# Per-head attention weights from a DRAM scratch, coarser loads and stores, and a reordered end, in a forward-and-backward kernel

## Chip, cores and metric

The kernel runs on one core of a Trainium2 chip. The metric is the device time in microseconds (us) of one execution. All data are bf16 in DRAM; sums are kept in f32 in PSUM.

## What is computed

The kernel computes a gated block and all its gradients, in one launch. With x of 2048 rows and D = 576 columns, 32 heads of 128 columns and 2048 cached keys and values per head:

```python
xn = layernorm(x)                                    # no affine part
q  = (xn @ wq) per head;  p = softmax(q @ K^T / sqrt(128));  o = p @ V
s  = concat(o) @ wo                                  # attention, 2048 x 576
g  = silu((sigmoid(xn @ w_gate) * (xn @ w_up)) @ w_down)   # MLP, inner size 4608
out = x + s * g
# and the gradients of out for x, K, V, wq, wo, w_gate, w_up, w_down, given grad_out
```

B_x is an input that the reference doesn't use.

## The kernel before

Rows are worked on in 16 tiles of 128 (`NT`, index `st` or `qt`); D = 576 is five tiles (`DT`), of which the last has 64 columns. Where weights lie with D on the partitions, this last tile is padded (`KPAD`): the 64 real rows lie in the upper half of the partitions, the lower half is zero. The stages follow each other on the one core:

1. MLP forward (lines 340 to 490): for 80 row steps (5 groups of columns of w_gate and w_up, 16 row tiles each; the first group is one chunk of 512 columns, the others two) TensorE makes `g_ps` and `u_ps`, ScalarE the sigmoid into `a_row`, VectorE the product into `h_row`. GpSimd stores both to DRAM (`h_d`, `a_d`, lines 472 and 473), with four buffers each. Beside it run the *guard* pieces (lines 249 to 281): SyncE loads K and wq into `x_all`, seven pieces ahead, and VectorE and ScalarE in turn square and sum them. They decide later whether the fast branch of attention, which has no row maximum, is safe. The order of this stage is written out by hand (`manual_schedule`).
2. The down projection (lines 505 to 548) and what is needed for the gate; the first head is prepared there too: `prep_kt`, `prep_wot` (TensorE turns wo of head 0 by five transposes) and `prep_qt`.
3. Attention, forward and backward, head by head (lines 594 to 868). A head has 32 slots: 16 of `main1` (scores, exponential, and a transpose of the row tile by DMA on SyncE, `PT`) and 16 of `main2` (dP, dS, and its transpose, `dST`). The tails `tail1` and `tail2` come six slots later and make O and dq, the sums over row tiles for dV and dK (`Partial`, line 744) are spread over the slots. `plan(h)` puts every other piece of work at a slot with `put`; a list scheduler then orders the instructions of each engine. GpSimd issues all plain loads and stores: per head K and V in quarters (line 177), wq in two loads (`load_wq`, 512 + 64 rows of 256 bytes), wo in two loads (`load_wo`), O and dq in stores of four row tiles each (`store_nat`, `G4 = 4`, lines 674 to 677). SyncE issues all DMA transposes: PT and dST, K and V (`turn_nat`), and wo of the next head (`turn_wot`, line 208), which lies in the single buffer `wo_h`.
4. The output product (lines 905 to 983): O of one row tile, turned by a DMA transpose (`load_oT`, line 584), times wo, whose rows have been loaded into dead buffers. Three buffers for the turned O, `oTs`, lie in KQ, in the rest of xnT and in `xn_all`. The loads of the second and third are held back by a one-element copy on GpSimd out of a row that was just loaded:

```python
loads[0] = row_loads(0)
for st in range(1, R0):
    nc.gpsimd.tensor_copy(oTs[st][0:1, 0, 0:1], loads[0][st % 3][0:1, 0:1])
    load_oT(oTs[st], st)
```

   TensorE works in the order: row tile 0 with those wo rows that are there early, row tile 1 with the same, row tile 0 with the late wo rows (those in Kn, Vn and dOn), then row tile 2, and so on.
5. The backward pass of the MLP in 18 blocks of 256 columns (lines 1055 to 1160).
6. The gradients of wq and wo and of xn through q, in eight groups of four heads (lines 1206 to 1262, `hg` = 0 to 7). A group has eight steps, in turn a product for dwq and one for dwo (`accumulate`, line 997); then for each row tile the product of the turned dq (`dqbT`) with the turned wq (`wqT`, in the place of `wdT2`) is added to `dxn` (line 1256). In the last two groups the rows are finished instead (`finish`, lines 1191 to 1203: six VectorE instructions and one ScalarE instruction per row tile, in a chain). Group 6 finishes row tiles 0 to 7, for which it also needs wq and dq of group 7 turned (`wqT2`, `dqbT2`); group 7 finishes 8 to 15. `wait_n` says after how many steps the rows begin. In stages 4 to 6 the order is by hand, except for ScalarE.

DMA transposes of a 128 x 2048 tile are 16 blocks of 128 x 128. A DMA on GpSimd is issued in the order of the program there, and one that has to wait holds up those behind it; the same holds on SyncE.

Of the kernel before, what the change touches and what calls it, by code (L numbers as in the profile page):

```python
# [9 lines left out]
bf = mybir.dt.bfloat16  # L10
# [56 lines left out]
def kernel(  # L67
# [40 lines left out]
    on2_d = dram.tile([S, HD], bf, name="on2_d")  # L108
    dq2_d = dram.tile([S, HD], bf, name="dq2_d")
    kvT_d = dram.tile([H, 2, P, S], bf, name="kvT_d")  # L110

# [13 lines left out]
    def zlow(t):  # L125
        if KPAD:
            nc.gpsimd.memset(t[:LO, DT - 1, :], 0.0)
# [9 lines left out]
    def acc_tile(dtype=f32):  # L137
        return acc_box[0](dtype)
# [12 lines left out]
    def new_head(h):  # L151
        hs = HeadState()
        hs.h = h
        hs.wq, hs.woT = wqs[h % 2], woTs[h % 2]
        hs.Kn = Kns[h % 2]
        hs.Vn, hs.VT, hs.KT, hs.QT, hs.dOT, hs.dOn, hs.Qn = Vn, VT, KT, QT, dOT, dOn, Qn
        return hs

    def load_wq(hs):
        hcols = slice(hs.h * P, (hs.h + 1) * P)  # L160
        nf = DT - 1 if KPAD else DT
        if nf:
            nc.gpsimd.dma_start(hs.wq[:, :nf, :], A_wq[:nf * P, hcols].rearrange("(i p) c -> p i c", p=P))
        if KPAD:
            nc.gpsimd.dma_start(hs.wq[LO:, nf, :], A_wq[nf * P:, hcols])

    def load_wo(hs):
        nf = (DT - 1) * P if KPAD else D
        rows = slice(hs.h * P, (hs.h + 1) * P)
        if nf:  # L170
            nc.gpsimd.dma_start(wo_h[:, :nf], A_wo[rows, :nf])
        if KPAD:
            nc.gpsimd.dma_start(wo_h[:, nf + LO:], A_wo[rows, nf:])

# [4 lines left out]
    def load_k(hs, c=0, n=1):  # L179
        load_kv(hs, hs.Kn, A_k_cache, c, n)  # L180
# [4 lines left out]
    def prep_loads(h):  # L185
        hs = new_head(h)
        load_wq(hs)
        load_wo(hs)
        load_k(hs)
        load_v(hs)  # L190
        return hs
# [5 lines left out]
    def prep_vt(hs):  # L197
        VTv = hs.VT[:].rearrange("p (t q) -> p t q", q=P)
        pe_transpose_blocks(lambda j: hs.Vn[:, j, :], 0, NT, lambda g, n: VTv[:, g:g + n, :], "v")

    def prep_wot(hs):
        pt = acc_tile(bf)
        for i in range(DT):
            nc.tensor.transpose(pt[:, i, :], wo_h[:, i * P:(i + 1) * P], ident[:])
        alt.copy(hs.woT[:], pt[:, :DT, :], eng="s")

    def turn_wot(hs):
        nc.sync.dma_start_transpose(hs.woT[:], wo_h[:])

# [24 lines left out]
    with tc.tile_pool(name="pa", bufs=1) as pa:  # L234
# [75 lines left out]
        with tc.tile_pool(name="a1w", bufs=1) as wp:  # L310
# [37 lines left out]
            with tc.tile_pool(name="a0", bufs=3) as sb0, tc.tile_pool(name="a0ps", bufs=2, space=PSUM) as ps0, \  # L348
# [51 lines left out]
                def load_wd():  # L400
                    f0 = wd_left.pop(0)
                    f1 = min(f0 + 3, FT)
                    nc.gpsimd.dma_start(wd_sb[:, f0:f1, :], B_w_down[f0 * P:f1 * P, :].rearrange("(t p) d -> p t d", p=P))

                todo = {"norm": list(range(min(LA + 2, L1), L1)), "turn": list(range(LA, L1)), "bn": list(range(L1, NT))}

# [25 lines left out]
                for n_row, (gi, st) in enumerate(rows_order):  # L432
# [41 lines left out]
                    if gi > 1 and st % 2 and wd_left:  # L474
                        load_wd()
                assert begin is not None
                while gk[0] < ntot:
# [3 lines left out]
                while wd_left:  # L481
                    load_wd()
                guard_end()
            NHV = min(NT, NT * D // (FT * P))
# [10 lines left out]
        pdT = tc.alloc_tile_pool(name="pdT", bufs=1, side="right")  # L495
        wqs = [pdT.tile([P, DT, P], bf, name=f"wq_h{b}") for b in range(2)]
        woTs = [pdT.tile([P, DT, P], bf, name=f"woT_h{b}") for b in range(2)]
        for t_ in wqs:
            zlow(t_)
        wo_h = pdT.tile([P, DT * P], bf, name="wo_h")  # L500
        if KPAD:
            nc.gpsimd.memset(wo_h[:, (DT - 1) * P:(DT - 1) * P + LO], 0.0)
        Qn = pdT.tile([P, NT, P], bf, name="Qn")
        VT, dOT = [pdT.tile([P, S], bf, name=nm) for nm in ("VT", "dOT")]
        heads_pre[0] = prep_loads(0)
        with tc.tile_pool(name="a2h", bufs=3) as hp, \
# [48 lines left out]
            prep_kt(heads_pre[0])  # L555
            prep_wot(heads_pre[0])
            for sc in range(S // CH):
# [29 lines left out]
    SKEW = 6  # L587
    G4 = min(4, NT)
    NSC = S // CH
# [3 lines left out]
    def attention(fast):  # L593
        with ExitStack() as es:
# [169 lines left out]
            def put(slot, cols, fn):  # L764
                units.setdefault(slot, []).append((cols, fn))
# [18 lines left out]
            def q(k):  # L784
                return min(k, NT - 1)

            def plan(h):
# [3 lines left out]
                if h:  # L791
                    put(pl, 0, lambda: heads.__setitem__(h, start_head(h)))
                    for c in range(4):
                        put(pl + q(c), 0, lambda c=c: load_k(hd(), c, 4))
                        put(pl + q(skew + 3 + c), 0, lambda c=c: load_v(hd(), c, 4))
                    put(pl + q(4), 0, lambda: load_wo(hd()))
                    put(pl + q(5), 0, lambda: load_wq(hd()))
                    put(pl + q(NTH + 3), 0, lambda: turn_nat(hd().KT, hd().Kn))
                    put(pl + q(skew + 4), 0, lambda: turn_wot(hd()))
                    for sc in range(NSC):  # L800
                        put(pl + q(skew + 4 + 2 * sc), DT * CH, lambda sc=sc: prep_qt(hd(), sc))
# [80 lines left out]
    with late("pc") as pc, late("pcf") as pcf, \  # L882
# [22 lines left out]
        with late("c1l3", 4) as ldp3, late("c1s", 2) as sb, \  # L905
# [34 lines left out]
            for st in range(1, R0):  # L940
                nc.gpsimd.tensor_copy(oTs[st][0:1, 0, 0:1], loads[0][st % 3][0:1, 0:1])
                load_oT(oTs[st], st)
# [217 lines left out]
        with late("c2w") as wp, late("c2b") as blk, late("c2s", 2) as sb, late("c2ps", 4, space=PSUM) as ps:  # L1160
# [45 lines left out]
            for hg in range(NHG):  # L1206
# [5 lines left out]
                nc.sync.dma_start_transpose(wqT, A_wq[:, cols])  # L1212
                for a in range(NTE if final else 0, NT, NQ):
                    turn_rows(dqbT, dqb, a, min(a + NQ, NT), HG)
                dwq = wp.tile([P, DT, HC], bf, name="dwq")
                for st in ends[:2]:
                    load_got(st)
                nsteps, step_n = 2 * HG, 0
                wait_n = min(5 if early else 2, nsteps - 2)
                todo_rows = list(ends)  # L1220
# [10 lines left out]
                for hl in range(HG):  # L1231
                    h = hg * HG + hl
                    lcols = slice(hl * P, (hl + 1) * P)
                    accumulate(ps.tile([P, WD], f32, name="acc"), dqb, xn_all, lcols, dqTs[h % 2])
                    nc.sync.dma_start_transpose(dwq[:, :, lcols], dqTs[h % 2][:])
                    if early and hl == min(1, HG - 1):
                        nc.sync.dma_start_transpose(wqT2[:], A_wq[:, (hg + 1) * HC:(hg + 2) * HC])
                        turn_rows(dqbT2, onqs[(hg + 1) % 2][1], 0, NTE, HG)
                    if final and hl == HG - 1:
                        store_T(out_4, cols, dwq)  # L1240
                    step_n += 1
                    ends_rows()
                    dwo = sb.tile([P, D], bf, name="dwo")
                    accumulate(ps.tile([P, WD], f32, name="acc"), onb, ds_all, lcols, dwo)
                    nc.gpsimd.dma_start(out_5[h * P:(h + 1) * P, :], dwo[:])  # L1245
                    step_n += 1
                    if hl < HG - 1:
                        ends_rows()
# [41 lines left out]
```

## Time and profile before

The time before is 4960.12 us, the median of three runs (4959.86 to 4975.73). The profiled execution has a span of 4944.8 us, with a mean granted TensorE clock of 0.997.

| | busy us | share of the span |
|---|---|---|
| TensorE matmul (PE) | 4874.4 | 99% |
| TensorE weight load (PEld) | 2893.5 | 59% |
| VectorE (DVE) | 2801.6 | 57% |
| ScalarE (ACT) | 2474.9 | 50% |
| GpSimd (POOL) | 842.3 | 17% |

The stages by the trace's order of time: MLP forward to 331 us, down projection to 482, attention to 3532, output product to about 3670, MLP backward to about 4540, and the last eight groups to the end. DMA moved 1097.68 MB in 3,048,180 packets, most of them the 256-byte packets of transposes. In the profile a row of a group of instructions has its line, engine, operation, what it writes and reads, the count, then busy us and mean ns of one, then the idle time of the engine just before these instructions and what ended it. Rows in order of time have the start, the length and the same names; the idle time before is in brackets. SPq and POOLq are the instruction queues of SyncE and GpSimd, where DMAs are issued; the length of a DMA there is the time of its issue, not of the transfer.

### The profile page before, as it was taken

How to read it: one execution, taken by the hardware profiler on the slowest of the kernel's cores; microseconds unless marked ns; L12 is line 12 of the kernel's file. 1: busy time of each engine (PE TensorE's matmuls, PEld its weight loads, DVE VectorE, ACT ScalarE, POOL GpSimd, SP SyncE). 2: the span in 40 equal slices, each digit the busy share in tenths (PEclk: the TensorE clock that was granted, in tenths of full speed). 3: DMA queues.
4: the chain of work that ended last, by engine and by line, in shares of the span. 5: the costliest groups of instructions: out<-in, count | busy, mean ns of one | idle time of the engine just before them, and what ended most of it. 6: DMA issues, size and time to landing. Idle time of an engine off the chain costs nothing. (4 is left out here: it accounts for less than half of the span.)

```text
span 4944.8 us, 101626 instructions
## 1 busy us (share of the span) xinstructions
PE 4874.4 (99%) x41029; PEld 2893.5 (59%) x41029; DVE 2801.6 (57%) x6554; ACT 2474.9 (50%) x4228; POOL 842.3 (17%) x1330
## 2 busy tenths in 40 slices
PE   9999999999999999999999999999899999999998
PEld 4445566666666666666666666666455555555554
DVE  4544666666566666666656656666434555553224
ACT  4432666766676676676676667667212111111111
POOL 3322111111111111111111111111221111111111
PEclk9999999999999999999999999999999999999999
DMA  7887999999999999999999999999999999997765
GB/s 260 274 202 175 219 222 227 227 228 226 228 231 226 228 228 232 225 228 229 224 229 231 230 222 231 225 226 231 216 221 238 224 226 223 234 235 185 205 175 131
DMA packets 3048180, 1097.68 MB, mean 222 GB/s; under 512 B 2951889, under 2 KB 2956114, under 8 KB 3047698
## 3 DMA queue, kind: packets, MB, share of 16 engines
q1 hardware_dynamic: 2948930, 771.66, 83.4%
q0 software_dynamic: 98160, 318.85, 20.3%
q8 instruction: 322, 5.28, 0.4%
q14 instruction: 160, 1.31, 0.1%
q10 hardware_dynamic: 608, 0.59, 0.0%
HBM read 175.31 MB, written 177.93 MB: 71 GB/s over the span
## 5 line engine op out<-in xcount | busy, mean ns | idle before, releaser
L654 ACT ACTIVATE Pq<-sp 128x1024 bf16<-128x1024 f32 x1024 | 1048.1, 1024 | 267.2 <-PE sp L636 258.1
L709 DVE SCALAR_TENSOR_TENSOR Pq<-dp,negdelta,Pq 128x1024 bf16<-128x1024 f32 x512 | 654.9, 1279 | 42.9 <-PE dp L706 42.9
L712 ACT ACTIVATE t<-dp,negdelta 128x1024 bf16<-128x1024 f32 x512 | 567.6, 1115 | 214.3 <-PE dp L706 199.8
L636 PE MATMUL sp<-KQ 128*128 128x512 bf16 x2048 | 609.7, 379 | 2.2 <-ACT Pq L654 2.1
L706 PE MATMUL dp<-VT,dOT 128*128 128x512 bf16 x2048 | 609.2, 379 | 2.3
L683 PEld LDWEIGHTS <-dST 128*128 128x128 bf16 x8192 | 508.1, 98 | 150.7 <-DMA dST<-Pq 9.9
L683 PEld LDWEIGHTS <-PT 128*128 128x128 bf16 x8192 | 500.2, 98 | 134.7 <-DMA PT<-Pq 14.0
L683 PE MATMUL acc<-Kn,dST 128*128 128x128 bf16 x8192 | 557.1, 219 | 5.7 <-DMA dST<-Pq 5.7
L683 PE MATMUL acc<-Vn,PT 128*128 128x128 bf16 x8192 | 542.4, 219 | 9.9 <-DMA PT<-Pq 9.6
L713 DVE TENSOR_TENSOR Pq<-t,Pq 128x1024 bf16<-128x1024 bf16 x512 | 354.5, 692 | 316.7 <-ACT t L712 306.2
L744 PE MATMUL acc<-Pq,dOn 128*128 128x512 bf16 x2048 | 531.7, 379 | 0.0
L744 PE MATMUL acc<-Pq,Qn 128*128 128x512 bf16 x2048 | 525.7, 379 | 0.0
L724 ACT ACTIVATE dq_n<-acc,rsc 128x128 bf16<-128x128 f32 x512 | 187.7, 367 | 331.5 <-PE acc L683 310.1
L1153 DVE TENSOR_TENSOR dxn<-acc,dxn 128x576 f32<-128x576 f32 x272 | 206.1, 758 | 248.2 <-PE acc L1053 248.2
L744 PEld LDWEIGHTS <-Qn 128*128 128x128 bf16 x2048 | 200.3, 98 | 240.4 <-issue 0.8
L744 PEld LDWEIGHTS <-dOn 128*128 128x128 bf16 x2048 | 199.0, 98 | 234.2 <-DVE dOn L669 0.3
L1115 ACT ACTIVATE ndh<-dh 128x512 bf16<-128x512 f32 x144 | 86.0, 597 | 452.5 <-DVE du_blk L1113 448.7
L641 DVE TENSOR_REDUCE rs_all<-rsp 128x1 f32<-128x2 f32 x512 | 78.3, 153 | 307.3 <-ACT Pq L654 295.8
L636 PEld LDWEIGHTS <-KQ 128*128 128x128 bf16 x2048 | 179.2, 98 | 124.1 <-issue 3.9
L706 PEld LDWEIGHTS <-dOT 128*128 128x128 bf16 x2048 | 178.7, 98 | 124.2 <-issue 11.7
L677 POOL DMA_DIRECT2D on_d<-o_n x128 | 97.3, 760 | 784.8 <-DVE junk L695 460.3
L677 POOL DMA_DIRECT2D dq_d<-dq_n x128 | 98.1, 766 | 716.9 <-ACT dq_n L724 677.1
(209 smaller groups left out, 6820.8 us busy)
## 6 DMA issues: line engine op xcount, KB each, us to landing
out_dram<-kvn POOLq DMA_DIRECT2D x64, 512.0 KB, 4.6
ah<-a_d POOLq DMA_DIRECT2D x18, 1024.0 KB, 9.5
ah<-h_d POOLq DMA_DIRECT2D x18, 1024.0 KB, 12.1
h_d<-h_row POOLq DMA_DIRECT2D x64, 256.0 KB, 3.4
a_d<-a_row POOLq DMA_DIRECT2D x64, 256.0 KB, 3.8
x_all<-in_A_k_cache_dram SPq DMA_DIRECT2D x64, 256.0 KB, 3.7
on_d<-o_n POOLq DMA_DIRECT2D x128, 128.0 KB, 4.7
kvT_d<-KQ POOLq DMA_DIRECT2D x32, 512.0 KB, 5.5
```

The costliest lines, as they stand in the source:

```text
L636: nc.tensor.matmul(sp[:, c * CH:(c + 1) * CH], lhsT=hs.QT[:, qt * P:(qt + 1) * P], rhs=hs.KT[:, hf * HW_ + c * CH: hf * HW_ + (c + 1) * CH ...
L654: nc.scalar.activation(Pq[:, hsl], sp[:], AF.Exp, scale=SCALE, accum_out=hs.rsp[:, hf:hf + 1])
L677: nc.gpsimd.dma_start(dst_d[q0 * P:(qt + 1) * P, hs.h * P:(hs.h + 1) * P].rearrange("(t p) d -> p t d", p=P), buf[:])
L683: nc.tensor.matmul(hs.acc[:, 0, :], lhsT=T[:, kt, :], rhs=rhs[:, kt, :], start=(kt == 0), stop=(kt == NT - 1))
L706: nc.tensor.matmul(dp[:, c * CH:(c + 1) * CH], lhsT=hs.dOT[:, qt * P:(qt + 1) * P], rhs=hs.VT[:, hf * HW_ + c * CH: hf * HW_ + (c + 1) * C ...
L709: nc.vector.scalar_tensor_tensor(Pq[:, hsl], dp[:], hs.negdelta[:, qt:qt + 1], Pq[:, hsl], op0=ALU.add, op1=ALU.mult)
L712: nc.scalar.activation(t[:], dp[:], AF.Identity, bias=hs.negdelta[:, qt:qt + 1], scale=1.0)
L713: nc.vector.tensor_tensor(Pq[:, hsl], t[:], Pq[:, hsl], op=ALU.mult)
L724: nc.scalar.activation(hs.dq_n[:, qt % G4, :], hs.acc[:, 0, :], AF.Copy, scale=hs.rsc[:, qt:qt + 1])
L744: nc.tensor.matmul(self.acc, lhsT=self.nat[:, qt, :], rhs=self.slabs[qt][:, cs], start=(qt == self.lo), stop=(qt == self.hi - 1))
L1115: nc.scalar.mul(ndh[:], dh[:], -1.0)
L1153: nc.vector.tensor_tensor(dxn[:, st, :], acc[:, :D], dxn[:, st, :], op=ALU.add)
```

## The change

Five edits, made together:

- wq of each head, padded, and wo of each head, turned, are put side by side into a new DRAM scratch `w2_d` during the MLP: for each pair of heads, GpSimd loads wq and SyncE turns wo by DMA transposes out of DRAM into an SBUF tile, and two row steps later GpSimd stores the tile (`w2_load`, `w2_store`; from row step 18 on, every second one, 16 pairs). In attention one load per head (`load_w2`) takes the place of four loads and a transpose; `wo_h`, `prep_wot` and `turn_wot` go. It is meant to take small transfers out of attention.
- K and V of the next head are loaded in halves instead of quarters.
- O and dq are stored eight row tiles at a time (`G4` = 8).
- In the output product the guard copy for row tile 1 goes; the one for row tile 2 stays.
- In group 6, wqT2 and dqbT2 are turned right after the first half of dqbT, and the second half of dqbT after the first two steps; the rows begin after 3 steps instead of 5 in group 6, and after 1 instead of 2 in group 7.

```diff
-    def load_wq(hs):
-        ...
-    def load_wo(hs):
-        ...
+    def load_w2(hs):
+        nc.gpsimd.dma_start(hs.w2[:], w2_d[hs.h])
...
-    def turn_wot(hs):
-        nc.sync.dma_start_transpose(hs.woT[:], wo_h[:])
...
+                def w2_load():
+                    if w2_left:
+                        hh = w2_left.pop(0)
+                        n = len(hh)
+                        t_ = sb0.tile([P, 2, 2, DT, P], bf, name="w2", bufs=2)
+                        cols = slice(hh[0] * P, (hh[-1] + 1) * P)
+                        for k in range(n):
+                            hc = slice(hh[k] * P, (hh[k] + 1) * P)
+                            if nf2:
+                                nc.gpsimd.dma_start(t_[:, k, 0, :nf2, :], A_wq[:nf2 * P, hc].rearrange("(i p) c -> p i c", p=P))
+                                nc.sync.dma_start_transpose(t_[:, k, 1, :nf2, :], A_wo[hc, :nf2 * P])
+                            if KPAD:
+                                nc.gpsimd.dma_start(t_[LO:, k, 0, nf2, :], A_wq[nf2 * P:, hc])
+                                nc.sync.dma_start_transpose(t_[:, k, 1, nf2, :], A_wo[hc, D - P:])
+                        w2_wait.append((t_, hh))
+
+                def w2_store():
+                    if w2_wait:
+                        t_, hh = w2_wait.pop(0)
+                        n = len(hh)
+                        if KPAD:
+                            nc.gpsimd.memset(t_[:LO, :n, :, nf2, :], 0.0)
+                        nc.gpsimd.dma_start(w2_d[hh[0]:hh[-1] + 1].rearrange("h p k i c -> p h (k i c)"),
+                                            t_[:, :n].rearrange("p h k i c -> p h (k i c)"))
...
+                    if n_row > NT and n_row % 2 == 0:
+                        w2_store()
+                        w2_load()
...
-    G4 = min(4, NT)
+    G4 = ldiv(NT, 8)
...
-                    for c in range(4):
-                        put(pl + q(c), 0, lambda c=c: load_k(hd(), c, 4))
-                        put(pl + q(skew + 3 + c), 0, lambda c=c: load_v(hd(), c, 4))
-                    put(pl + q(4), 0, lambda: load_wo(hd()))
-                    put(pl + q(5), 0, lambda: load_wq(hd()))
+                    for c in range(2):
+                        put(pl + q(2 * c), 0, lambda c=c: load_k(hd(), c, 2))
+                        put(pl + q(skew + 3 + 2 * c), 0, lambda c=c: load_v(hd(), c, 2))
+                    put(pl + q(4), 0, lambda: load_w2(hd()))
                     put(pl + q(NTH + 3), 0, lambda: turn_nat(hd().KT, hd().Kn))
-                    put(pl + q(skew + 4), 0, lambda: turn_wot(hd()))
...
             for st in range(1, R0):
-                nc.gpsimd.tensor_copy(oTs[st][0:1, 0, 0:1], loads[0][st % 3][0:1, 0:1])
+                if st > 1:
+                    nc.gpsimd.tensor_copy(oTs[st][0:1, 0, 0:1], loads[0][st % 3][0:1, 0:1])
                 load_oT(oTs[st], st)
...
-                for a in range(NTE if final else 0, NT, NQ):
-                    turn_rows(dqbT, dqb, a, min(a + NQ, NT), HG)
+                def turn_dq(a, b):
+                    for a_ in range(a, b, NQ):
+                        turn_rows(dqbT, dqb, a_, min(a_ + NQ, b), HG)
+                turn_dq(NTE if final else 0, NTE if early else NT)
+                if early:
+                    nc.sync.dma_start_transpose(wqT2[:], A_wq[:, (hg + 1) * HC:(hg + 2) * HC])
+                    turn_rows(dqbT2, onqs[(hg + 1) % 2][1], 0, NTE, HG)
...
-                wait_n = min(5 if early else 2, nsteps - 2)
+                wait_n = min(3 if early else 1, nsteps - 2)
...
                     if early and hl == min(1, HG - 1):
-                        nc.sync.dma_start_transpose(wqT2[:], A_wq[:, (hg + 1) * HC:(hg + 2) * HC])
-                        turn_rows(dqbT2, onqs[(hg + 1) % 2][1], 0, NTE, HG)
+                        turn_dq(NTE, NT)
```

## The prediction

> **What bounds the kernel now.** I read the page first, then TensorE's waits, then the order of time around each of its gaps, then stretches of the first 520 us. The page:
>
> ```profile
> span 4944.8 us, 101626 instructions
> PE 4874.4 (99%) x41029; PEld 2893.5 (59%) x41029; DVE 2801.6 (57%) x6554; ACT 2474.9 (50%) x4228; POOL 842.3 (17%) x1330
> ...
> q1 hardware_dynamic: 2948930, 771.66, 83.4%
> q0 software_dynamic: 98160, 318.85, 20.3%
> ```
>
> TensorE is the bound: 4944.8 - 4874.4 leaves 70 us in which it is idle, 11 of them after its last matmul and 9 before its first. Inside attention (488 to 3532 us) stretches of 100 us show it busy 99.9 us, and 16 matmuls of 128 columns start 0.89 us apart in total, 55.6 ns each. Nothing that only lightens DMA or GpSimd can speed that part up, beyond the single gaps. These are the largest waits of TensorE (wait in us, times, longest):
>
> ```profile
> PE acc L957 <- DMA xnT<-on_d: 10.8, 1, 10.8
> PE pt L378 <- ACT x_all L372: 10.5, 4, 8.6
> PE acc L683 <- DMA PT<-Pq: 9.6, 6, 3.6
> PE acc L683 <- DMA dST<-Pq: 5.7, 5, 3.0
> PE acc L1053 <- DMA dqbT<-dqb: 3.9, 1, 3.9
> ```
>
> So the whole question is which of some 55 us of gaps the change closes, and whether it opens new ones in the MLP, where it puts new transfers.
>
> **What the Trainium skill says.** "TensorE: Matmul & The Clock Gate", Part 1: 55.6 ns from start to start of warm 128-column matmuls, and half the clock after an idle window of about 3.4 us. The trace agrees: 55.6 ns, and the eight matmuls after the 3.89 us gap below took 2.10 us instead of 1.15, so a long gap costs one to two us more than itself. "DMA: Bandwidth & Descriptors", Rules for kernel authors: coalesce many small transfers. The same page, Issuing engines are not separate DMA queues: transfers from SyncE and GpSimd interleave on the same 16 engines. The page's DMA rows fit: a share above 1 where both queues work. The same page, Where 436 GB/s comes from: a ceiling of 435 GB/s; the best 20 us stretch here moved 369.
>
> **Attention: stores by eight, K and V in halves, one weight load.** The compiled order of TensorE and VectorE inside attention is the same in both kernels. GpSimd loses, per head, 4 of 8 stores of 0.76 us, 4 of 8 K/V loads of 0.54 us and three of four weight loads; its 784.8 and 716.9 us of idle time before the stores say that nobody waits for it: 0. SyncE loses one woT transpose of 5 blocks per head, of 34 x 16 + 5 = 549, 1% of the transposes: 0 in steady state, since TensorE has no idle time there. But at the start of attention it matters (SyncE's order of time, then TensorE's; start, length, what, and in brackets the wait):
>
> ```profile
> 488.72 1.20 SPq L208 DMA_TRANSPOSE woT_h<-wo_h  x1
> 490.33 7.50 SPq L630 DMA_TRANSPOSE PT<-Pq  x3
> 498.35 1.20 SPq L208 DMA_TRANSPOSE woT_h<-wo_h  x1
> 499.60 22.47 SPq L630 DMA_TRANSPOSE PT<-Pq  x9
> ```
>
> ```profile
> 506.40 0.40 PE L683 MATMUL acc<-Vn,PT 128*128 128x128 bf16 x4 [3.63 <-DMA PT<-Pq]
> ```
>
> SyncE issues a PT every 2.5 us (22.47 / 9), slower than the exponentials (about 2.1 us a row), so each woT ahead of it delays all that follow, the first PT by 1.6 us and the fourth by about 3. TensorE's gaps here are 1.28 + 3.63 us and cost about 1.5 us of slow clock. Without the two woT I take -3.5 us (between -1, if the pace of the DMA engines and not of SyncE's issue sets it, and -6). The five TensorE transposes of prep_wot go too, 0.27 us with a wait of 0.18: -0.5.
>
> **The step from attention to the output product.** This is the change at the guard copies: the one for row tile 1 goes.
>
> ```profile
> 3539.26 4.67 SPq L584 DMA_TRANSPOSE xnT<-on_d  x1
> 3544.02 12.11 SPq L584 DMA_TRANSPOSE xn_all<-on_d  x1
> ```
>
> ```profile
> 3549.23 5.75 PE L957 MATMUL acc<-dsT,xnT 128*128 128x512 bf16 x34 [10.76 <-DMA xnT<-on_d]
> ...
> 3560.77 4.33 PE L957 MATMUL acc<-dsT,xn_all 128*128 128x512 bf16 x34 [2.12 <-DMA xn_all<-on_d]
> ```
>
> SyncE is done with dST at 3525.9 (the last group of eight starts at 3506.71 and takes 19.18) and then does nothing until 3539.26, when GpSimd's one-element copy, which waits for a row load, lets xnT go. Without that copy its waits are on stores of O that landed long before, so xnT should be issued at about 3529, ten us sooner. An earlier transpose of the same size (KQ from on_d, issued at 3501.74) took 7 us to land, so xnT is there at 3537, and TensorE, done with the early wo rows of row tile 0 at 3538.5 (3536.84 + 1.63), goes on at once. The two wo passes for row tile 1 take 6 us, to 3544.5. Then row tile 0 needs the wo rows in Kn, Vn and dOn; their issue (3540.3 to 3542.6) is unchanged and dOn was used at 3557.8; with 7 to 8 us to land, as the transfers beside it show, about 3550. So a gap of 3 to 6 us is put in place of the one of 10.8. xn_all still waits for its guard copy at 3539.8, but xnT no longer stands ahead of it: issued at 3540 instead of 3544 and without xnT's traffic, it lands 8 to 10 us later, at about 3550. The matmuls on xn_all then begin at about 3551 instead of 3560.77: -9.5 us (from -5, if the landing of xn_all remains 16 us behind its issue, to -11).
>
> **The last two head groups.** Here SyncE's order and two thresholds change: wqT2 and the first half of dqbT2 are turned before the second half of dqbT, and the final rows begin after three steps instead of five, and after one instead of two.
>
> ```profile
> 4840.52 2.51 SPq L1237 DMA_TRANSPOSE wqT<-in_A_wq_dram  x1
> 4843.13 4.37 SPq L1048 DMA_TRANSPOSE dqbT<-dqb  x1
> ```
>
> ```profile
> 4849.29 2.10 PE L1053 MATMUL acc<-wqT,dqbT 128*128 128x512 bf16 x8 [3.89 <-DMA dqbT<-dqb]
> ```
>
> ```profile
> 4901.56 0.76 DVE L1192 SCALAR_TENSOR_TENSOR tot<-acc,dxn 128x576 f32<-128x576 f32 x1 [8.06 <-PE acc L1053]
> ```
>
> VectorE's chain per final row is 4.35 us (rows started at 4851.43, 4855.91, 4860.21, and so on), eight rows 34.8 us in each group. In the last group it starts at 4901.56 and ends at 4936.4, and the span ends 8.4 us after. So the end is set by when those chains can start. Group 6: SyncE begins at 4824.85 (3.75 us for wdT's place, two dqbT pieces of 2.26, 2.51, 4.37 = 15.2 us to 4840) and the last data lands 1.8 us after, as before; by the DMA rate (146 blocks landed in 24.4 us, 0.167 each; now 104) at 4842.2. TensorE comes there after three steps of 3.92 us, at 4836.4, and waits about 4.8 us, a gap in place of the one of 3.89. But from there its remaining work is five steps (19.6), eight double rows (15.7), eight single rows (7.8) and some 1 to 2 us of slow clock, and VectorE's chain, begun at 4844.3, ends at 4879, before the single rows need it: the gaps of 2.23 and 2.79 go. Group 6 ends at 4886.3 instead of 4892.5. Last group: wdT's place 2.06 + a piece 2.26 + 1.7 to land = 4892.3; one step ends at 4890.2; the first row is there at 4893.3 instead of 4901.56, and TensorE supplies one row per 4.9 us after the first four, so VectorE stays the bound: end of chain at 4928.1. -8 us; I take -7.5, between -3 (a longer wait for dqbT2) and -9.
>
> **What the change adds in the MLP.** 32 heads x (147 KB of wq, 5 blocks of wo turned, a store of 328 KB), in 16 pairs, one per two rows from row 18 (72 us) to row 50 (204 us). GpSimd gets 2 x 0.76 + 2 x 0.55 + a store of 0.75 and a fill of 0.3, 3.7 us per two rows of 4.31 us, where it has 2.2 to 3: fits. DMA: q1 cost 83.4% x 16 x 4944.8 us / 2,948,930 = 22.4 ns a packet, a block is 128 packets, so 160 blocks are 160 x 128 x 22.4 ns / 16 = 29 us of all engines; q0 cost 20.3% x 4944.8 / 318.85 = 3.15 us per MB, and 15.2 MB are 48 us. That is 77 us in 132, a share of 0.58 on top of this:
>
> ```profile
> 160.00:180.00 20.00, 20.00 (x94) 9.10 (x93) 11.32 (x18) 10.05 (x19) 6.56 (x11) 1.00 0.88 284
> ```
>
> (the last two columns are DMA share and GB/s). Together 1.37, or 275 + 20 MB / 132 us = 425 GB/s. Attention sustains a share of 1.12 to 1.19; the best stretch is 369 GB/s. So transfers fall behind by 19 us (by bytes) to 24 us (by share). New waits: the store on GpSimd waits for the transposes, and h_d, a_d of the next rows are queued behind it; the transposes on SyncE wait for the store two pairs back, and the guard loads are queued behind them, for which VectorE and ScalarE wait in order, and TensorE for those. The buffers are four rows (17 us) and a lead of seven guard loads of 2.41 us (154.19 / 64), 17 us. So 2 to 7 us come through, or none if queues overlap better than I allow; I take +3, range 0 to +20.
>
> **Sum.** -3.5 - 0.5 - 9.5 - 7.5 + 3 = -18 us: 4960.1 - 18 = 4942.
>
> **Rivals.** (a) Gains remain in part: xn_all lands late (-5), the end gives -4, attention's start -2, the MLP costs 3: -8, 4952. For it: each gap closed has another transfer right behind it. (b) Slower: the MLP's buffers are used up and each of 16 stores holds GpSimd for some 2.5 us that TensorE sees: +40 - 18 = +22, 4982. For it: 425 GB/s asked; against: three levels of buffering. (c) Also other attention gaps (808, 3477, 3511, 3526 us; some 10 us with their slow clock) go: 4930.
>
> **Chances.** Main case 0.46, (c) 0.12, (a) 0.27, (b) 0.15. Faster by over 0.3% (under 4945.2) 0.58, same 0.27, slower 0.15. The range from 4927 to 4972 takes in (a), (c) and the MLP's cost up to its bound.
>
> **What would show it.** xnT issued within some us of the last dST and no gap over 6 us there; VectorE's last chain of eight rows starting some 69 us after the start of group 6 (now 4901.56 - 4824.66 = 76.9); little or no gap on PT in the first 20 us of attention; TensorE still busy for 20.00 of 20 us between 80 and 200 us. New waits of VectorE or ScalarE on x_all loads, or of GpSimd on the transposes of A_wo that reach TensorE, would make the prediction wrong.

## The result, and the profile after

The changed kernel takes 5007.05 us (median of 4, 5000.44 to 5015.37) against 4959.99 (4 runs, 4953.28 to 4975.73) before, a ratio of 1.0091 (95% interval 1.0063 to 1.0120): slower by some 47 us, where 4942 had been predicted. The page of the changed kernel:

```profile
span 5013.6 us, 100928 instructions
PE 4903.9 (98%) x41024; PEld 2899.2 (58%) x41024; DVE 2797.9 (56%) x6554; ACT 2470.7 (49%) x4227; POOL 702.9 (14%) x1074
...
q1 hardware_dynamic: 2950626, 771.83, 82.5%
q0 software_dynamic: 96432, 335.09, 21.5%
```

TensorE is busy 30 us longer with the same work (so at a slower clock somewhere) and idle 40 us more. Its largest waits now:

```profile
PE g_ps L456 <- ACT a_row L463: 39.0, 15, 5.3
PE acc L690 <- DMA dST<-Pq: 15.5, 14, 3.0
PE pt L357 <- ACT x_all L351: 10.7, 4, 8.7
PE acc L1059 <- DMA dqbT<-dqb: 8.3, 2, 5.7
PE acc L541 <- DMA hT_st<-h_d: 4.8, 2, 3.6
PE acc L963 <- DMA Vn<-in_A_wo_dram: 4.0, 1, 4.0
PE acc L963 <- issue: 3.8, 1, 3.8
```

The first row did not exist before, and it is the MLP. Two stretches of it; the columns end with granted clock, DMA share and GB/s:

```profile
160.00:180.00 20.00, 17.15 (x71) 7.36 (x71) 9.74 (x16) 6.97 (x14) 11.70 (x19) 0.91 1.13 286
180.00:200.00 20.00, 14.16 (x58) 5.95 (x57) 5.73 (x9) 5.39 (x10) 10.12 (x17) 0.91 1.12 282
```

TensorE works 17.2 and 14.2 of 20 us, at a clock of 0.91, while the DMA share has gone up from 0.88 to 1.13 and the bytes have not gone up at all (284 GB/s before). The fifteen waits add up to 39.0 us; the MLP ends at 390.6 us instead of 331.3. The other 20 us are matmuls at half the clock: at ten of the fifteen gaps, of 2.49 to 5.27 us, the granted clock went to 0.5 for 3.4 or 6.8 us, 37.5 us in all. The prediction names an idle window of about 3.4 us for this; here shorter gaps were enough, in e5 one of 2.06 us. One of them on TensorE, where five matmuls otherwise take 1.24 us:

```profile
237.11 1.71 PE L456 MATMUL g_ps<-wg_sb,xnT 128*128 128x512 bf16 x5 [2.49 <-ACT a_row L463]
238.61 2.34 PE L458 MATMUL u_ps<-wu_sb,xnT 128*128 128x512 bf16 x5
```

The stages of all kernels that follow, from the starts of TensorE's first instruction of each stage (us; the time is the median of the runs, the stages are those of the one profiled execution; the down projection takes in the preparation of the first head; the MLP backward with the first six head groups takes 1147.2 in all but one, where it takes 1148.0):

| kernel | MLP ends | down projection | attention | output product | last two groups | time |
|---|---|---|---|---|---|---|
| before | 331.3 | 151.9 | 3048.9 | 145.4 | 120.1 | 4960.0 |
| after | 390.6 | 158.2 | 3055.3 | 147.9 | 114.5 | 5007.1 |
| e1 no scratch | 331.2 | 151.9 | 3080.2 | 145.4 | 112.7 | 4973.3 |
| e2 before + building | 390.4 | 153.3 | 3048.9 | 153.1 | 118.7 | 5014.6 |
| e3 wq on SyncE | 384.3 | 159.5 | 3045.1 | 148.3 | 116.4 | 5002.0 |
| e4 three w2 buffers | 384.3 | 158.5 | 3049.4 | 145.7 | 112.9 | 4999.6 |
| e5 wo not turned | 350.3 | 160.6 | 3056.6 | 149.6 | 113.8 | 4967.8 |
| e6 wq in long rows | 380.7 | 152.6 | 3041.1 | 148.5 | 114.2 | 5002.3 |
| e7 after, quarters | 396.6 | 158.4 | 3048.8 | 147.1 | 113.8 | 5000.6 |
| e8 end + guard copy | 331.1 | 151.9 | 3047.4 | 145.0 | 113.7 | 4943.5 |
| e9 e8, fill as guard | 331.1 | 151.9 | 3061.7 | 149.2 | 115.1 | 4949.0 |
| e10 end only | 330.8 | 151.9 | 3061.0 | 153.4 | 114.5 | 4954.5 |
| e11 guard copy only | 331.2 | 151.9 | 3052.2 | 143.9 | 120.2 | 4952.0 |
| e12 turned from SBUF | 393.3 | 157.8 | 3050.5 | 147.2 | 114.5 | 5007.6 |
| e13 e3 and e4 | 377.9 | 160.1 | 3052.9 | 147.4 | 113.9 | 5005.6 |
| e14 half the pace | 366.0 | 159.6 | 3052.6 | 150.3 | 115.8 | 4989.3 |

Between the two profiles of before and after the stages differ by +59.3, +6.3, +6.5, +2.4, 0 and -5.7 (in unrounded times), together the 68.8 us between the two spans. The medians differ by 47 only: the profiled execution of before took 4946.6, near the low end of its kernel (4943.9 to 4967.9 in 36 further runs), that of after was the slowest of its four.

Where does the MLP's wait come from? ScalarE's waits between 80 and 290 us have one large row, and GpSimd's order of time (idle before in brackets) shows what stands behind it:

```profile
ACT a_row L463 <- DMA a_d<-a_row: 123.1, 29, 9.1
```

```profile
111.35 0.55 POOL L480 DMA_DIRECT2D h_d<-h_row  x1
117.60 0.54 POOL L481 DMA_DIRECT2D a_d<-a_row  x1 [5.70 <-DMA w_d<-w]
118.57 0.52 POOL L409 MEMSET w<- 64x512 bf16 x1 [0.43 <-DMA w<-in_A_wo_dram]
119.45 0.72 POOL L410 DMA_DIRECT2D w_d<-w  x1 [0.37 <-POOL w L409]
```

The sigmoid waits for an a_row buffer whose store has not landed. That store was issued late, because it waited for the landing of the scratch's store eight DMAs earlier: in the trace GpSimd's DMAs use eight completion semaphores in turn (numbers 111 to 118). And everything lands late: in the page's list of issues a K piece of the guard takes 11.6 us from issue to landing (3.7 before), and h_d, after and then before:

```profile
h_d<-h_row POOLq DMA_DIRECT2D x64, 256.0 KB, 6.9
...
h_d<-h_row POOLq DMA_DIRECT2D x64, 256.0 KB, 3.4
```

So there were three candidates: the chain over GpSimd's semaphores (L), the chain over two w2 buffers (B), and DMA engines with nothing left to give (C). A fourth is rival (b) of the prediction, the scratch's fill and store on GpSimd, which wait for the turned blocks and hold up the stores of rows behind them (16.6 us in nine waits between 80 and 290 us); no run was made for it alone.

The rest of the profile answers the prediction's other lines. The start of attention, SyncE and then TensorE:

```profile
553.19 15.46 SPq L637 DMA_TRANSPOSE PT<-Pq  x6
```

```profile
564.06 0.23 PE L690 MATMUL acc<-Vn,PT 128*128 128x128 bf16 x1 [0.83 <-DMA PT<-Pq]
```

No woT stands among the PT any more, and 0.83 us of gap are left of 4.9. From attention to the output product, SyncE and TensorE:

```profile
3600.98 5.21 SPq L591 DMA_TRANSPOSE xnT<-on_d  x1
3616.27 7.61 SPq L591 DMA_TRANSPOSE xn_all<-on_d  x1
```

```profile
3604.09 3.32 PE L963 MATMUL acc<-dsT,KQ 128*128 128x512 bf16 x25 [0.84 <-PE acc L751]
3611.21 2.16 PE L963 MATMUL acc<-dsT,KQ 128*128 128x64 bf16 x9 [3.81 <-issue]
...
3623.97 0.90 PE L963 MATMUL acc<-Kn,KQ 128*128 128x512 bf16 x6 [1.68 <-DMA Kn<-in_A_wo_dram]
3628.85 1.60 PE L963 MATMUL acc<-Vn,KQ 128*128 128x512 bf16 x6 [3.99 <-DMA Vn<-in_A_wo_dram]
...
3633.16 6.39 PE L963 MATMUL acc<-dsT,xn_all 128*128 128x512 bf16 x34 [1.27 <-DMA xn_all<-on_d]
```

xnT is issued 3 us before the stage begins instead of 7 after, and nobody waits for it. But three new gaps of 3.8, 1.7 and 4.0 us stand in its place, the first of them with no wait shown, and xn_all comes 29.1 us after the stage's start (28.7 before). The end, SyncE, TensorE, VectorE:

```profile
4910.63 4.98 SPq L1054 DMA_TRANSPOSE dqbT<-dqb  x1
```

```profile
4917.71 2.10 PE L1059 MATMUL acc<-wqT,dqbT 128*128 128x512 bf16 x8 [5.68 <-DMA dqbT<-dqb]
```

```profile
4969.69 0.76 DVE L1198 SCALAR_TENSOR_TENSOR tot<-acc,dxn 128x576 f32<-128x576 f32 x1 [7.36 <-PE acc L1059]
```

The last chain of eight rows starts 70.6 us after group 6 (at 4899.13), where it was 76.9 before and 69 was predicted.

### The profile page after: what moved, and what is told of

Same layout as the page of the kernel before. It is cut to its first block, busy times and chain, and to the rows that moved or that the text cites. A ratio compares the mean times of both kernels' runs of the same rounds, so it can differ in the third digit from the quotient of the medians.

```text
span 5013.6 us, 100928 instructions
## 1 busy us (share of the span) xinstructions
PE 4903.9 (98%) x41024; PEld 2899.2 (58%) x41024; DVE 2797.9 (56%) x6554; ACT 2470.7 (49%) x4227; POOL 702.9 (14%) x1074
## 5 line engine op out<-in xcount | busy, mean ns | idle before, releaser
L456 PE MATMUL g_ps<-wg_sb,xnT 128*128 128x512 bf16 x720 | 188.7, 395 | 39.0 <-ACT a_row L463 39.0
L464 DVE TENSOR_TENSOR h_row<-u_ps,a_row 128x512 bf16<-128x512 f32 x144 | 99.0, 691 | 218.7 <-ACT a_row L463 144.2
## 6 DMA issues: line engine op xcount, KB each, us to landing
x_all<-in_A_k_cache_dram SPq DMA_DIRECT2D x64, 256.0 KB, 11.6
```

Of the source, the lines that this page charges most:

```text
L456: nc.tensor.matmul(g_ps[:], lhsT=xnT[:, i, srows], rhs=wg_sb[:, i, fs], start=(i == 0), stop=(i == DT - 1))
```

## The experiments

**Which edit costs what: e1, e2.** One leaves the scratch out of the changed kernel, one puts it alone into the kernel before.

```diff
 e1 (against after)
-        load_w2(hs)
+        load_wq(hs)
+        load_wo(hs)
...
-                    if n_row > NT and n_row % 2 == 0:
-                        w2_store()
-                        w2_load()
-    G4 = ldiv(NT, 8)
+    G4 = min(4, NT)
 e2 (against before)
+                    if n_row > NT and n_row % 2 == 0:
+                        w2_store()
+                        w2_load()
```

> The changed kernel without the scratch: wq and wo are loaded and wo is turned per head as before, and (for lack of SBUF beside wo_h) O and dq are stored by four; K and V in halves, the missing guard copy and the reordered end stay. If the scratch built during the MLP is the cause, the MLP ends at 331 us again instead of 391, the down projection takes 156 us instead of 162, and the time is 4945 to 4957, at or below the kernel before. If the attention part or the output product cost something of their own, the time stays above 4965.

> The kernel before plus the building of the scratch alone (nobody reads it). If the building is the cause: MLP end at 388 to 393 us, down projection some 5 us longer, time 5015 to 5025 (before + 60). If the loss came from reading the scratch in attention or from the other edits: at most 4975.

e2: 5014.57 us, ratio 1.0121 (1.0100 to 1.0141), MLP end 390.4. The building alone costs all of the loss and more. e1: the MLP is back at 331.2, but the time is 4973.25, ratio 1.0028 (1.0016 to 1.0040), which is the last line of its expectation: attention takes 3080.2 us. So one of the other edits costs time once the scratch is gone.

**The two chains of waits, one at a time: e3, e4.**

```diff
 e3
-    nc.gpsimd.dma_start(t_[:, k, 0, :nf2, :], A_wq[:nf2 * P, hc].rearrange("(i p) c -> p i c", p=P))
+    nc.sync.dma_start(t_[:, k, 0, :nf2, :], A_wq[:nf2 * P, hc].rearrange("(i p) c -> p i c", p=P))
-    nc.gpsimd.dma_start(t_[LO:, k, 0, nf2, :], A_wq[nf2 * P:, hc])
+    nc.sync.dma_start(t_[LO:, k, 0, nf2, :], A_wq[nf2 * P:, hc])
 e4
-    t_ = sb0.tile([P, 2, 2, DT, P], bf, name="w2", bufs=2)
+    t_ = sb0.tile([P, 2, 2, DT, P], bf, name="w2", bufs=3)
```

> The changed kernel with the four wq loads per pair issued on SyncE instead of GpSimd: same bytes, same packets, same buffers. Theory L (GpSimd's DMAs take eight completion semaphores in turn, nine DMAs per two rows, so the last a_d of a pair waits until the w2 store of the pair before has landed, and the next store can only follow that: period = landing of the store, 9.4 us, + 3 us, against 8.63 us for two rows): five DMAs per two rows break the chain, MLP end at 335 to 350 us, time 4950 to 4970. Theory B (two w2 buffers: transposes wait for the store two pairs back): MLP end near 375, time 4990. Theory C (the DMA engines are full, share 0.98): MLP end at 385 to 395, time 5005.

> The changed kernel with three w2 buffers instead of two. Theory L: the chain over the eight completion semaphores is untouched, MLP end at 380 to 391, time 5000 to 5007. Theory B: transposes need not wait for the last store, MLP end at 340 to 355, time 4955 to 4975. Theory C: 390, 5007.

e3: 5002.02 us, ratio 1.0090 (1.0065 to 1.0114). e4: 4999.59, ratio 1.0071 (1.0047 to 1.0095). The MLP ends at 384.3 in both, 6 us earlier than after, which is no more than single profiles of one design differ (e2 390.4, e7 396.6). L and B each fall as the one cause of the whole loss.

**What fills the engines: e5, e6, e12.** e5 loads wo without turning it, e6 loads wq in long rows, e12 turns wo out of SBUF instead of DRAM.

```diff
 e5
-    nc.sync.dma_start_transpose(t_[:, k, 1, :nf2, :], A_wo[hc, :nf2 * P])
+    nc.sync.dma_start(t_[:, k, 1, :nf2, :], A_wo[hc, :nf2 * P].rearrange("p (i c) -> p i c", c=P))
 e6
-    nc.gpsimd.dma_start(t_[:, k, 0, :nf2, :], A_wq[:nf2 * P, hc].rearrange("(i p) c -> p i c", p=P))
-    nc.gpsimd.dma_start(t_[LO:, k, 0, nf2, :], A_wq[nf2 * P:, hc])
+    nc.gpsimd.dma_start(t_[:, k, 0, :, :], A_wq[:P, :DT * P].rearrange("p (i c) -> p i c", c=P))
 e12
+    r_ = sb0.tile([P, 2, D], bf, name="wo_r", bufs=2)
+    nc.sync.dma_start(r_[:, :len(hh)], A_wo[hh[0] * P:(hh[-1] + 1) * P, :].rearrange("(k p) d -> p k d", p=P))
...
-    nc.sync.dma_start_transpose(t_[:, k, 1, :nf2, :], A_wo[hc, :nf2 * P])
+    nc.sync.dma_start_transpose(t_[:, k, 1, :nf2, :], r_[:, k, :nf2 * P])
```

> The changed kernel with the wo rows loaded plainly in the MLP instead of turned (left out: the turning, so the scratch holds wo unturned); same bytes, same queues, same number of DMAs and waits. Theory T (the DMA engines are full, and the turned loads are what fills them: 1,280 packets per two rows at 33 to 51 ns are 2.6 to 4.1 us of the 12.5 us that two rows now take): MLP end at 335 to 350 us, time 4950 to 4968. Theory Y (bytes: 425 GB/s asked): unchanged, 385 to 391. Theory Q (wq's rows of 256 bytes): 375 to 391.

> The changed kernel with each head's wq loaded as one piece of 128 rows of 1,280 bytes in place of 576 rows of 256 bytes (left out: the right columns, the scratch holds other weights); the bytes are about the same, GpSimd issues 7 instead of 9 DMAs per two rows. Theory Q (the 256-byte rows fill the engines): MLP end at 340 to 360 us. Theory T: 375 to 388 us, time 4990 to 5005. Theory Y: 385 to 391.

> The changed kernel with the wo rows loaded plainly into SBUF one pair ahead, and turned from there instead of from DRAM. Theory M (a turned block costs about twice as much beside plain traffic, 0.34 us against 0.17 in attention, whatever it reads from): the plain load comes on top, MLP end at 388 to 405 us, time 5005 to 5020. Theory D (it is reading single rows out of DRAM that makes it dear): the turned blocks fall to 0.17 us, MLP end at 360 to 375, time 4975 to 4990.

e5: 4967.79 us, ratio 1.0020 (1.0007 to 1.0033), MLP end 350.3: theory T, at the upper edge of its range. The same two stretches of e5 as shown of after:

```profile
160.00:180.00 20.00, 20.00 (x94) 9.09 (x93) 10.14 (x18) 8.82 (x17) 13.57 (x23) 1.00 1.00 366
180.00:200.00 20.00, 18.39 (x85) 8.22 (x84) 9.68 (x17) 8.00 (x15) 14.05 (x23) 1.00 1.04 378
```

With the same bytes asked, the engines now move 366 and 378 GB/s instead of 286 and 282. So the bytes were not the limit; turning wo costs 40 of the 59 us, by the price of the turned blocks or by the waits for their landing, which e5 does not separate. e6: 5002.25 us, ratio 1.0088 (1.0054 to 1.0121), MLP end 380.7: wq's short rows matter by 10 us at most. e12: 5007.64 us, ratio 1.0098 (1.0077 to 1.0118), MLP end 393.3, the numbers of theory M. But its trace does not bear out the reason. Between 100 and 280 us the 256-byte packets of the turned blocks took 35.4 ns on average in after and 23.0 in e12 (22.1 in the attention of before, 1000 to 3000 us), as theory D had it, and they landed sooner. The first line is of after, the second of e12, and the third, SyncE's largest wait in e12 (80 to 290 us), shows what came in their place:

```profile
w<-in_A_wo_dram SPq DMA_TRANSPOSE x52, 10.6
...
w<-wo_r SPq DMA_TRANSPOSE x53, 6.5
...
SPq L406 <- DMA wo_r<-in_A_wo_dram: 39.8, 13, 6.9
```

SyncE waits for the plain load before each turn, with the guard's loads queued behind, and GpSimd waits 73.6 us for the turned blocks. So e12 does not show that turning out of SBUF costs as much; it put another wait in the place of a cheaper block.

**Both chains away, and half the pace: e13, e14.** Since e3 and e4 take one chain away each, the two might bind in turn. e13 is e3 and e4 together.

```diff
 e14
-    w2_left = [list(range(h, min(h + 2, H))) for h in range(0, H, 2)]
+    w2_left = [[h] for h in range(H)]
-                    if n_row > NT and n_row % 2 == 0:
+                    if n_row > NT - 5 and n_row % 2 == 0:
```

> The changed kernel with both reliefs at once: the wq loads on SyncE (five GpSimd DMAs per two rows instead of nine) and three w2 buffers. If the two chains of waits bind in turn, so that taking away one only uncovers the other (theory L with B), the MLP ends at 335 to 350 us and the time is 4950 to 4970. If the engines have no more to give (theory C), it still ends at 378 to 392 us, time 4993 to 5008.

> The changed kernel with the scratch built at half the pace: one head per two row steps, from step 12, so over 64 steps instead of 32; the same loads, turns and bytes in all. Theory C: two rows alone take 8.63 us at a share of 0.78, that is 6.1 us of full engines (share 1.10); a pair of heads adds 12.3 - 6.1 = 6.2 us, a head 3.1; two rows with one head then ask 9.2 us against 8.63: 32 times 0.6 us are 19 us less some 11 that the buffers take up, MLP end at 338 to 352 us, time 4950 to 4968. If the cost hangs on the amount and not on the pace (each load or store costs TensorE the same wherever it lies), the MLP ends at 380 to 391 us again, 4995 to 5007. If only chains of waits had bound it, 331 to 334 us, 4943 to 4950.

e13: 5005.60 us, ratio 1.0092 (1.0072 to 1.0113), MLP end 377.9. Of 59 us some 46 stay with neither chain left. ScalarE's waits in e13, from 50 to 400 us, have only moved in part to the guard's loads, and on GpSimd the wait for the turned blocks, 16.6 us in after, has become the largest:

```profile
ACT x_all L247 <- DMA x_all<-in_A_k_cache_dram: 59.2, 13, 8.0
ACT a_row L463 <- DMA a_d<-a_row: 51.7, 14, 6.3
...
POOL w L409 <- DMA w<-in_A_wo_dram: 107.9, 14, 12.7
```

Transfers land in 4.6 to 6.9 us there (100 to 280 us), where after had 8.3 to 11.6. So e13 rules out that L and B alone bound the MLP, and does not show theory C: the hold on GpSimd can bind in their place.

e14 loads one head per two row steps, from step 12 on: 4989.31 us, ratio 1.0052 (1.0034 to 1.0070), MLP end 366.0, so 35 us lost instead of 59. That misses every line of its expectation, and for a reason that none of them had. GpSimd, SyncE and TensorE at the end of its MLP:

```profile
347.29 0.30 POOL L409 MEMSET w<- 64x256 bf16 x1 [20.94 <-DMA w<-in_A_wo_dram]
```

```profile
317.00 13.90 SPq L501 DMA_TRANSPOSE x_all<-h_d  x1
...
343.62 1.21 SPq L398 DMA_TRANSPOSE w<-in_A_wo_dram  x1
```

```profile
366.03 6.29 PE L541 MATMUL acc<-wd_sb,x_all 128*128 128x512 bf16 x29 [23.61 <-DVE h_row L464]
```

The last heads' turns were queued on SyncE behind the next stage's transposes and behind a load that waits for the guard's result; GpSimd's fill waited for them for 20.94 us, with the last a_d stores behind it. Without this one wait of 23.6 us the MLP would, by subtraction, have ended at 342.4, within theory C's 338 to 352, but no run shows it. Up to 326 us TensorE has five gaps over 0.8 us in this part, 7.7 us in all, where after had fourteen over 0.8, 38.6 us. So it is not the amount alone that sets the cost. Pace and place are not separated: 29 of the 64 turns are now issued after 204 us, and the last ones at the end of the MLP, where the other traffic is lighter (before has a DMA share of 0.69 at 260 to 280 us and 0.47 at 280 to 300).

**K and V in halves: e7, e8.** e7 is the changed kernel with quarters, e8 is e1 with quarters, that is, the kernel before with only the end and the guard copy changed.

```diff
 e7 (against after), e8 (against e1)
-                    for c in range(2):
-                        put(pl + q(2 * c), 0, lambda c=c: load_k(hd(), c, 2))
-                        put(pl + q(skew + 3 + 2 * c), 0, lambda c=c: load_v(hd(), c, 2))
+                    for c in range(4):
+                        put(pl + q(c), 0, lambda c=c: load_k(hd(), c, 4))
+                        put(pl + q(skew + 3 + c), 0, lambda c=c: load_v(hd(), c, 4))
```

> The changed kernel with K and V loaded in quarters again. If the halves are what made attention slower in the run without the scratch (3075.8 us from its first score to the output product, against 3044.5 before), quarters give the changed kernel an attention of 3038 to 3043 us instead of 3051.9 in its profile and 3042 to 3046 in the two variants of its MLP, and a time of 4995 to 5003. If the halves do nothing here, 3042 to 3052 and 5000 to 5009.

> The kernel before plus the reordered end and without the guard copy for row tile 1; weights, K and V in quarters, and stores by four as before. If halves without the scratch cost some 20 us (the run without the scratch took 4973), this takes 4948 to 4955: the end gives -5.6 to -7.5, the output product 0 (145.4 us, as in the runs of the changed kernel). If the halves are not the cause and the loss lies in the other edits, it stays near 4970.

e8: 4943.45 us, ratio 0.9974 (0.9967 to 0.9980), faster than both kernels and 27 us (by the ratios) to 30 us (by the medians) below e1, from which it differs by the quarters alone; its attention takes 3047.4 us against 3080.2. e7: 5000.56 us, ratio 1.0084 (1.0062 to 1.0107): with the scratch, halves or quarters make no difference that the intervals separate. Most of e1's loss is gaps on PT (25.3 us between 560 and 3520 us, e8 3.1). Near one of them, GpSimd in e1 and then at the same place in before:

```profile
1548.91 0.55 POOL L171 DMA_DIRECT2D wo_h<-in_A_wo_dram  x1 [13.02 <-DMA woT_h<-wo_h]
...
1550.00 1.07 POOL L177 DMA_DIRECT2D Kn<-in_A_k_cache_dram  x2
```

```profile
1545.45 0.56 POOL L171 DMA_DIRECT2D wo_h<-in_A_wo_dram  x1 [12.97 <-DMA woT_h<-wo_h]
...
1546.55 1.60 POOL L177 DMA_DIRECT2D Kn<-in_A_k_cache_dram  x3
...
1548.89 0.54 POOL L177 DMA_DIRECT2D Kn<-in_A_k_cache_dram  x1
```

The wo load waits 13 us for the turn of the wo before it, and K is queued behind it; a PT shortly after is held in its issue for 8.81 us on SyncE (6.70 before). In the changed kernel this wait is gone with `wo_h`. But the wait is the same in before, and the four quarters too start within 2.3 us, so the burst by itself does not tell e1 from e8. Why halves lose without the scratch is not shown.

**The end and the guard copy, each alone: e10, e11, e9.** e10 has the diff of the end, e11 the one of the guard copy. e9 is e8 with a guard that waits for no load:

```diff
 e9 (against e8)
+            if R0 > 1:
+                nc.gpsimd.memset(oTs[1][0:1, 0, 0:1], 0.0)
             loads[0] = row_loads(0)
```

> The kernel before with the reordered end alone. By the stage times of the profiles (120.1 us before, 112.7 to 116.4 after, from the start of group 6) the end gives -4 to -7 of the 13 us that the end and the missing guard copy gave together: 4949 to 4954. If it gives all of it: 4942 to 4946.

> The kernel before without the guard copy for row tile 1 alone. By the two profiles the output product does not change (145.4 and 145.0 us): 4954 to 4960. But another run with the copy had a gap of 19.45 us on xnT and took 153.1 us; if that is as usual as 145.4, removing the copy gives -4 to -7: 4949 to 4953.

> The kernel before with the reordered end, and the turn of row tile 1 of the output product held back by a one-element fill on GpSimd, its first instruction after attention, in place of the guard copy (which waits for a row load). Theory F: where the copy is simply gone, the transpose is in flight while TensorE and GpSimd fetch the instructions of the new stage, and the fetch takes some 4 us longer (3.77 us of idle time ended by 'issue', and Kn, Vn loaded 4 us later), which eats the gain. Then here that gap is under 1.5 us, the wait for xnT 4 to 6 us, and the output product takes 140 to 143 us instead of 145.0; time 4939 to 4943. If the fetch has nothing to do with the transposes, the gap of about 3.8 us stays and the wait for xnT is added: 147 to 150 us, 4946 to 4950.

e10: 4954.46 us, ratio 0.9990 (0.9982 to 0.9999). e11: 4952.00, ratio 0.9992 (0.9985 to 0.9999). Each gives 3 to 6 us, whether by medians or ratios; e8, which has both, gives 13, somewhat more than the sum, within the intervals' reach. The largest wait of e10, which still has the copy:

```profile
PE acc L957 <- DMA xnT<-on_d: 19.7, 1, 19.7
```

and the two largest in the output product of e8, which has not:

```profile
PE acc L958 <- issue: 5.3, 2, 3.8
PE acc L958 <- DMA Vn<-in_A_wo_dram: 3.2, 1, 3.2
```

With the copy the output product takes 145.4 (before), 153.1 (e2) and 153.4 us (e10), without it 145.4 (e1), 145.0 (e8) and 143.9 (e11) in kernels without the scratch. e9: 4949.02 us, ratio 0.9985 (0.9975 to 0.9996), output product 149.2, TensorE:

```profile
3547.52 1.88 PE L960 MATMUL acc<-dsT,KQ 128*128 128x512 bf16 x14 [0.20 <-issue]
...
3558.08 6.43 PE L960 MATMUL acc<-dsT,xnT 128*128 128x512 bf16 x34 [7.21 <-DMA xnT<-on_d]
...
3570.74 1.60 PE L960 MATMUL acc<-Vn,KQ 128*128 128x512 bf16 x6 [4.02 <-DMA Vn<-in_A_wo_dram]
```

The gap without a shown wait falls from 3.8 to 0.2 us when the transpose starts later, as theory F said, so the two hang together. But the wait for xnT is longer than it said and Vn comes no sooner: 6 us slower than e8, with a time and an output product in the ranges of the other line. Theory F holds for the gap and fails as a remedy.

## Why the prediction was wrong

**The MLP (+3 predicted, +59.3 measured; the failing step).** The demand was seen, and so were the waits it would cause. What failed is "So 2 to 7 us come through", by three of its terms. First, the price of a turned block: 22.4 ns a packet from the page's mean of the whole span, 128 x 22.4 / 16 = 0.18 us. In the MLP of after the packets took 35.4 ns, 0.28 us a block. An estimate from the times is higher: e5 against after gives 40.3 us for 160 blocks, and the plain loads that e5 has instead, 5.2 MB at some 370 GB/s, are 14 more, about 54 / 160 = 0.34 us, waits included. (The Trainium skill, "DMA: Bandwidth & Descriptors", Latency and other measured facts, gives 261 GB/s for a DMA transpose with a non-contiguous middle dimension; a block of 32.8 KB in 0.28 us is 117 GB/s, in 0.18 us 182. The measurement decides.) Second, the capacity: 369 GB/s had been seen without turned loads, and a share of 1.12 to 1.19 in attention with hardly any plain ones. Here the mix moved 276 GB/s at a share of 1.10 (the mean from 100 to 280 us). The share does not tell how much is moved: e14, with fewer turned blocks in the time, moved 319 GB/s at 1.08 (100 to 300 us). Third, the buffers: they were credited against the whole backlog; they carried TensorE from 79.7 us, GpSimd's first load of wq, to 109.8, and from then on it had about one gap for each pair of heads. And a cost that the prediction itself had named for other gaps was not counted here: fifteen gaps, 39.0 us, bring 20 us of slow clock.

**Rival (b)** named the right side and, by its own arithmetic, nearly the right waits: 16 times 2.5 us, against 15 with a mean of 2.6. It left out the clock. Its cause, the hold on GpSimd, stands untested: in e3 and e13, where the other chains are broken, GpSimd waits 119.2 and 107.9 us for the turned blocks. Whether full engines or this hold set the pace of the changed kernel stays open; storing each pair a few row steps later, on top of e13, would separate them. Its argument against ("three levels of buffering") should have been dropped: here the buffers were used up 30 us after GpSimd's first load.

**Attention in steady state (0).** 3055.3 us against 3048.9 lies within what profiles of the two designs show (3041.1 to 3056.6 with the scratch, 3047.4 to 3061.7 without, halves apart). As a sum right; as a reason wrong: "TensorE has no idle time there" does not mean that transfers are free, since halves without the scratch cost 27 to 30 us.

**Start of attention (-3.5 and -0.5).** The gaps on PT shrank as predicted, by 4.1 us. But e8, whose start of attention is that of the kernel before, has no PT gap over 0.8 us there, and e2, e9, e10 and e11 have one of 1.8 to 2.0. Before's 4.9 us were one execution's. e8 has both woT among its PT and no gap, so that little of the -3.5 can be put down to their going. What comes back in every kernel that reads the scratch is the wait ahead of the scores, 1.0 to 1.1 us instead of 2.1.

**Output product (-9.5).** The mechanism was right, xnT early and no wait for it, and so was roughly the worth: e11 against before -4 (ratio) to -6 us (medians), e8 against e10 -8 to -11. The profile of after shows none of it, because the profile of before happened to have the wait at 10.8 where two other runs had 19.5 and 19.7, and because of two things that the step left out: the 3.8 us gap at the change of stage, and Kn and Vn, issued 12.5 us after the stage's start instead of 8.2, where the step took their issue for unchanged (GpSimd, too, stood 7.15 us with no wait shown, 3.13 before).

**The end (-7.5).** Right: -5.7 in the two profiles, the wait at group 6 5.7 instead of 4.8 (the prediction's own times for it, 4836.4 and 4842.2, give 5.8), the last chain at 70.6 instead of 69, the gaps on tot and dxn gone. By e10's times -3 (medians) to -5 (ratio), with an interval from -0.5 to -9.

**What was left out altogether.** The down projection is 6 us longer in nearly every kernel with the whole change: its first turned h rows land late (waits of 1.3 and 3.6 us). With the building alone, in e2, the stage is 1.4 us longer. Why the reading kernels lose more was not looked into.

Left open is why a turned block cost more here than in attention. That it is the reading of single rows out of DRAM beside plain traffic is what e12's packets suggest (35.4 ns out of DRAM, 23.0 out of SBUF); as a remedy e12 failed, by its other waits.

## What to carry to other kernels

Before putting background transfers into a stage, price each kind in the mix it will meet, and compare with the rate that such a mix has sustained: a share above 1 is no sign of room, and buffers carry only the first few steps. Look for what queues behind each new wait: with two chains of waits taken away, 46 of 59 us stayed and another wait had grown. Spreading the same transfers over twice the steps cut the loss from 59 to 35 us. Compare the profiled execution's time with the timed ones before counting its gaps: a gap that one execution happens to have is no saving, and one that it happens to lack is no proof against a saving. Of this change the reordered end and the missing guard copy are worth keeping, by themselves: 4943.45 us, ratio 0.9974.

## What was not expected of the hardware

- A DMA transpose of 128 x 128 out of DRAM beside plain transfers took 0.28 us of all engines by its packets (35.4 ns each), against 0.18 in attention and in e12 out of SBUF (22.1 and 23.0 ns). With the turned loads one stretch moved 286 GB/s, with plain ones 366.
- Gaps of 2.06 us (e5) and 2.49 us (after) were followed by 3.4 us at half the TensorE clock.
- A DMA on GpSimd can wait for one that it has nothing to do with: eight completion semaphores in turn, so a_d waited 5.70 us for the landing of w_d.
- At the change of stage after attention TensorE stood for 2.6 to 5.4 us with no wait shown in the twelve kernels in which the transpose of xnT had just been issued, and for 0.2 to 1.2 us in the four in which it had not (before, e2, e9, e10). The traces' packets of the kind "instruction" (DMA queues 8 and 14) point to the fetching of instructions: from 3 us before the stage to 8 after it, the longest pause between two of them is 3.9 to 7.0 us in the twelve and 2.1 to 2.5 in the four. No run tests it further.
